# GpSimd's gather, token numbers and low parts of w1 in another order and with fewer waits, and TensorE's instruction pages ended at chosen places

## The chip, the cores and the metric

The kernel runs on one core of one Trainium2 chip. A core has five engines that run side by side, each with its own list of instructions, and that wait for each other through semaphores: TensorE (PE in the profile; its weight loads are PEld), VectorE (DVE), ScalarE (ACT), GpSimd (POOL) and SyncE (SP), which here only starts transfers. The metric is the time of one execution on the device in microseconds; less is better.

## What is computed

Attention in chunks of 64 keys, then a mixture of experts with two levels of routing. `N` is 4608 tokens, `D` 512, `F` 1024; there are 4 groups of 4 experts.

```python
scores = scale * (q_c @ k_c.T)              # per batch, head and chunk of 64
attn = softmax(scores);  x = attn @ v_c     # x becomes [4608, 512]
g_idx = argmax(x @ w_group);  g_w = softmax(x @ w_group)[g_idx]
e_idx = argmax(x @ w_expert[g_idx]);  e_w = softmax(...)[e_idx]
h = maximum(x @ w1[g, e], 0)
out = g_w * e_w * (h @ w2[g, e])            # each token by its one expert
```

## The kernel before

**Two halves.** The first half is one straight list of instructions for each engine, written by a recorder (`Recorder`), that finds by itself which instruction must wait for which; the second half is a loop over blocks of up to 256 tokens of one expert. In the profile every recorded instruction has the line of the recorder's `play`, L309, so the first half is told apart by tiles.

**The first half** handles 36 tiles of 128 tokens in a software pipeline. In turn t TensorE computes the scores of tile t+1 (`b`, tiles `qk`), transposes the exponentials of tile t-1 (`c`, tile `pr`), takes every second turn products for the router (`xT` with `wg`, or `lt` with `cs`), computes the weighted sum of tile t-2 (`p`, tiles `va` and `pT`) and transposes x of tile t-3 (`x`). VectorE normalises a tile's x (`n`: `rc`, then x), subtracts the maximum (`s`: `m`, then `pr`) and does the routing in pieces (`more`). The last turns and what is added to single turns stand in two tables of letters, `TAIL` and `EXTRA`.

**GpSimd** has three kinds of work here. It writes the token numbers into the last columns of x, one column for each tile (`tensor_copy`, CAST in the profile). It scatters the rows of x by expert into the DRAM array `xs`, one indirect DMA for each tile (L752; tiles come in groups of four, a group has one of the buffers `xl`, `x0`, `x1`, `x2`, used again four groups later). And it prepares the first expert: it starts the loads of its w1 and w2 (letter F, `w1r` and `w2r`), gathers its first 256 tokens from `xs` into `xg0r` (F2 and F3), and computes the low parts of w1 (letter P, eight pieces, `w1l` = `w1r` - `w1h`; ScalarE writes `w1h` just before).

**What the recorder makes wait.** All of `xs` is one entry in the recorder's book. A scatter counts as a reader of the entry, a gather as a writer:

```python
def scatter_x(pos, g, i):
    R.gpsimd.do(..., [pos, x, ("xs", (0, 1, 0, 1))], [], "s%d" % (g % 4), g)
...
R.gpsimd.do(lambda e: e.dma_start(xg0[:, j, :], xs[ds(st["r", j], P), :]),
            [], [xg0[:, j, :], ("xs", (0, 1, 0, 1))], "g%d" % j)
```

So a gather waits for all scatters in front of it in the list, the second gather for the first, and every later scatter for the second gather, each until the transfer has landed. GpSimd works through its list in order.

**TensorE's list** of the first half has 1810 entries. An f32 product takes four instruction slots (two passes, each a weight load and a matmul), a transpose or a product of another type two, a wait that stands alone one. The list runs through without regard to where a block of 256 slots ends.

Of the kernel before, what the change touches and what calls it, by code (L numbers as in the profile page):

```python
# [19 lines left out]
P = 128  # L20
# [26 lines left out]
EXTRA = {3: "C0", 4: "Z0", 5: "Z1", 6: "Z2", 7: "Z3", 8: "Z4",  # L47
         24: "F0", 25: "F1", 27: "P0 P1", 28: "F4", 29: "F2 F3", 30: "P2 P3 F5", 31: "P4 P5 P6"}
TAIL = ("b34 n30 s33 c32 m1 p31 m2 e33 x30 b35 n31 s34 m1 c33 P7 p32 m2 e34 x31 36 n32 s35 B0 c34 p33 17 e35 m1 n33 x32 27 W0"
        " p34 c35 n34 B1 m2 W1 x33 W2 p35 n35 m2 x34 X0 x35 X1 m3 R0 R1 37 18 m3 y0 y1 y2 W3 W4 W5 W6 W7 y3 R2 y4 y5 y6 L0 28 m2 m1 L1 m4 H0 y7"  # L50
# [63 lines left out]
BASE, TOP = 16512, 229376  # L114
LATE = 25600


class Op:
    def __init__(self, eng, fn, lane):
        self.eng, self.fn, self.lane, self.waits, self.inc = eng, fn, lane, [], False  # L120


class Recorder:
# [4 lines left out]
    def __init__(self, tc):  # L128
        self.tc = tc
        self.ops = {e: [] for e in self.ENGINES}  # L130
        self.seen = {e: {} for e in self.ENGINES}
        self.hist = {}
        self.lanes = {}
        self.alias = {}
        self.live = {}
        for e in self.ENGINES:
            setattr(self, e, Engine(self, e))
# [16 lines left out]

    def add(self, eng, fn, reads, writes, lane=None, group=None):
        op = Op(eng, fn, lane)
        op.plain = False
        op.at = len(self.ops[eng])
        need = []
        acc = [(a, False) for a in reads] + [(a, True) for a in writes]  # L160
# [97 lines left out]
    def wait(self, o, val):  # L258
        return (self.sem[o.eng], o.count) if o.lane is None else (self.sem[o.lane], 16 * val)

    def play(self, name, eng):
        for op in self.ops[name]:
            last = op.waits[-1:] if op.plain else []
            for w in op.waits[:len(op.waits) - len(last)]:
                eng.wait_ge(*self.wait(*w))
            if op.fn is None:
                continue
            z = op.fn(eng)
            for w in last:
                z._wait_ge(*self.wait(*w))  # L270
            if op.lane is not None:
                z.then_inc(self.sem[op.lane], 16)
            elif op.inc:
                z.then_inc(self.sem[name], 1)

# [15 lines left out]
class Engine:  # L291
    def __init__(self, rec, name):
        self.rec, self.name = rec, name

    def do(self, fn, reads=(), writes=(), lane=None, group=None):
        return self.rec.add(self.name, fn, list(reads), list(writes), lane, group)

    def __getattr__(self, op):
        def f(*args, **kw):
            named = dict(kw)  # L300
            lane, group = named.pop("lane", None), named.pop("group", None)
            aps = lambda z: [a for a in z if hasattr(a, "tensor") and hasattr(a, "ap")]
            if "out" in named:
                writes, reads = [named["out"]], aps(args) + aps(v for k, v in named.items() if k != "out")
            else:
                writes, reads = [args[0]], aps(args[1:]) + aps(named.values())
            reads = [a for a in reads if a.space != DRAM]
            writes = [a for a in writes if a.space != DRAM]
            z = self.do(lambda e: getattr(e, op)(*args, **named), reads, writes, lane, group)  # L309
            z.plain = True  # L310
            return z
        return f
# [3 lines left out]
def moe_kernel(tc, qk, v, wgs, w1, w2, cst, out):  # L316
# [4 lines left out]
    with ExitStack() as ctx:  # L321
# [114 lines left out]
        with ExitStack() as c1:  # L436
# [87 lines left out]
            def stage_b(t):  # L524
                s = st.setdefault(t, {})
                T = st["T", t // 2][:, t % 2]
                sc = scb[t % 2]
                for hp in range(4):
# [30 lines left out]
            def stage_pv(t):  # L559
                s = st[t]  # L560
                pT = s["pT"]
                W = HD + 1
                o = scb[0] if t == NT - 2 else ob
                for hp in range(4):
                    for x, c, rows, cols in TILES:
# [3 lines left out]
            def stage_norm(t):  # L569
# [10 lines left out]
                if i == 0:  # L580
                    st["x", g] = xl if g % 4 == GL % 4 else xbufs[g % 4 - 1]
                R.gpsimd.tensor_copy(st["x", g][:, i, D:D + 1].bitcast(I32), cs[:, C_TID + t:C_TID + t + 1])
                x = st["x", g][:, i, 0:D]
# [214 lines left out]
            def first_loads(i):  # L798
# [873 lines left out]
```

## Time and profile before

| | |
|---|---|
| median of 3 runs | 624.8 us (624.0 to 625.17) |
| profiled execution | 627.61 us, its span 626.0 us |
| PE busy | 583.8 us, 93% |
| DVE, ACT, POOL busy | 364.3, 263.1, 161.2 us |
| mean granted TensorE clock | 0.968 of full speed |
| data moved | 128.24 MB, mean 205 GB/s |

The span runs from the first to the last instruction of the profiled execution; 1.6 us of its time lie around it. The first half, with attention and routing, ends at about 172 us; the loop over experts takes the rest. Busy shares are means over both. An engine counts as busy while an instruction runs on it; "idle before" is the time in front of an instruction in which its engine ran nothing, and the name behind it is what ended that time. "issue" stands for idle time for which no other engine and no transfer is found. The granted clock is given as a share of 2.4 GHz; in this trace it is 1.0 or 0.5 at any one time.

### The profile page before, as it was taken

The page shows a single profiled execution, that of the slowest core. Times are in us where ns is not written, and L with a number is a line of the kernel's source. Part 1 is how long each engine was busy: PE and PEld are TensorE (multiplying, and loading weights), DVE is VectorE, ACT ScalarE, POOL GpSimd, SP SyncE. Part 2 cuts the span into 40 slices and gives each one's busy share as a digit, 9 for nine tenths or more (in the row PEclk, how much of TensorE's full clock was granted, in tenths as well). Part 3 has the DMA queues.
Part 4 walks back from the last instruction along what each step waited for, and adds up shares of the span by engine and source line. Part 5 has one row for each costly group of instructions (what it writes and reads, how often), then busy time and mean ns, then how long its engine had stood idle before and what let it go on. Part 6 is the DMA issues. An engine that isn't in the chain of part 4 may idle for free.

```text
span 626.0 us, 16004 instructions
## 1 busy us (share of the span) xinstructions
PE 583.8 (93%) x5711; PEld 503.1 (80%) x5712; DVE 364.3 (58%) x688; ACT 263.1 (42%) x367; POOL 161.2 (26%) x279
## 2 busy tenths in 40 slices
PE   6897989957899999989999999999999999999995
PEld 4766767745779799878889899989989988898984
DVE  4586769863876672127497674725525578854311
ACT  2464445743444461125475362625215365552111
POOL 0002324348342311221333212221111124311120
PEclk9798889985999999999999999999999999999999
DMA  8987997729639984115489954451712686931110
GB/s 299 422 278 258 372 363 229 228 77 286 173 108 323 328 300 171 68 30 200 142 298 339 301 191 180 171 206 63 281 50 89 238 317 206 339 102 67 34 38 30
DMA packets 43103, 128.24 MB, mean 205 GB/s; under 512 B 4590, under 2 KB 4974, under 8 KB 41136
## 3 DMA queue, kind: packets, MB, share of 16 engines
q1 hardware_dynamic: 32192, 93.93, 43.4%
q0 software_dynamic: 10864, 33.64, 15.3%
q8 instruction: 35, 0.57, 0.4%
q14 instruction: 12, 0.10, 0.0%
HBM read 106.40 MB, written 21.93 MB: 205 GB/s over the span
## 4 chain that ended last, share of the span: by engine, by line
PE 77%; DMA 10%; DVE 5%; issue 4%; POOL 2%; SPq 1%; ACT 1%; POOLq 0%; ACTq 0%; DVEq 0%
PE banks L1109 29%; PE banks L1094 22%; PE banks L309 14%; PE banks L1078 5%; DMA xs<-xl,pos 3%; DMA w1r<-in_moe_w_dram 2%; DMA xgr<-xs 2%; PE banks L994 2%; DMA out_dram<-xl,io__154 1%; DMA qk<-in_qk_dram 1%; PE banks L1040 1%; PE banks L1063 1%; PE banks L1010 1%; DVE big L309 1%; DVE m L309 1%
## 5 line engine op out<-in xcount | busy, mean ns | idle before, releaser
L1094 PE MATMUL banks<-big,w1h 128*128 128x256 f32 x896 | 128.1, 283 | 1.6 <-issue 1.6
L1094 PEld LDWEIGHTS banks<-big,w1h 128*128 128x128 f32 x896 | 117.3, 192 | 3.0 <-issue 2.0
L1255 ACT ACTIVATE big<-banks 128x512 fp32r<-128x512 f32 x58 | 34.5, 597 | 158.6 <-PE banks L1094 105.3
L1109 PE MATMUL banks<-big,big 128*128 128x512 f32 x360 | 84.6, 393 | 0.0
L1585 POOL DMA_INDIRECT out_dram<-xl,io__154 x37 | 41.1, 1111 | 154.8 <-DVE xl L1321 144.0
L1109 PEld LDWEIGHTS banks<-big,big 128*128 128x128 f32 x360 | 66.5, 188 | 14.4 <-ACT big L1305 0.7
L1354 DVE SCALAR_TENSOR_TENSOR big<-banks,big 128x512 fp32r<-128x512 f32 x54 | 36.1, 687 | 64.5 <-ACT big L1255 64.1
L1094 PE MATMUL banks<-big,w1l 128*128 128x256 f32 x448 | 72.3, 283 | 0.6 <-DVE w1l L1331 0.6
L1109 PE MATMUL banks<-w2h,big 128*128 128x512 f32 x288 | 71.2, 393 | 1.5 <-ACT big L1255 1.4
L1331 DVE TENSOR_TENSOR w1l<-w1r,w1h 128x2048 fp32r<-128x2048 f32 x28 | 63.1, 2290 | 16.1 <-ACT w1h L1242 14.3
L1321 DVE TENSOR_SCALAR xl<-banks,io__154 128x512 f32<-128x512 f32 x33 | 24.7, 748 | 67.5 <-PE banks L1109 66.0
L1109 PEld LDWEIGHTS banks<-w2h,big 128*128 128x128 f32 x288 | 53.1, 188 | 13.0 <-ACT big L1255 1.8
L1094 PEld LDWEIGHTS banks<-big,w1l 128*128 128x128 f32 x448 | 61.9, 192 | 0.8 <-DVE w1l L1331 0.8
L1242 ACT CAST w1h<-w1r 128x2048 fp32r<-128x2048 f32 x28 | 52.1, 1903 | 6.7 <-DMA w1r<-in_moe_w_dram 4.9
L309 PE MATMUL banks<-va,pT 64*64 64x65 f32 x1152 | 30.0, 247 | 13.9 <-DVE x L309 6.9
L309 PEld LDWEIGHTS banks<-va,pT 64*64 64x64 f32 x1152 | 24.2, 154 | 23.2 <-DVE x L309 7.9
L309 PE MATMUL banks<-qk 64*64 64x64 f32 x1152 | 29.4, 233 | 11.6 <-issue 7.8
L309 PEld LDWEIGHTS banks<-qk 64*64 64x64 f32 x1152 | 23.0, 141 | 20.2 <-issue 11.0
L1335 DVE TENSOR_TENSOR w2l<-w2r,w2h 128x1024 fp32r<-128x1024 f32 x32 | 37.1, 1218 | 1.8 <-ACT w2h L1274 1.2
L309 ACT COPY pT<-banks 128x512 f32<-128x512 f32 x36 | 21.1, 585 | 36.4 <-PE banks L309 35.8
L1109 PE MATMUL banks<-w2l,big 128*128 128x512 f32 x144 | 35.6, 389 | 0.0
L752 POOL DMA_INDIRECT xs<-x,pos x24 | 24.8, 1033 | 39.7 <-DVE pos L309 27.0
(218 smaller groups left out, 898.6 us busy)
## 6 DMA issues: line engine op xcount, KB each, us to landing
w1r<-in_moe_w_dram SPq DMA_DIRECT2D x30, 1024.0 KB
w2r<-in_moe_w_dram SPq DMA_DIRECT2D x30, 1024.0 KB
qk<-in_qk_dram SPq DMA_DIRECT2D x15, 1024.0 KB, 15.3
xgr<-xs POOLq DMA_DIRECT2D x38, 257.0 KB, 5.2
va<-in_v_dram SPq DMA_DIRECT2D x24, 390.0 KB
qk<-in_qk_dram SPq DMA_DIRECT2D x6, 512.0 KB, 8.6
w1r<-in_moe_w_dram POOLq DMA_DIRECT2D x2, 1024.0 KB, 9.7
w2r<-in_moe_w_dram POOLq DMA_DIRECT2D x2, 1024.0 KB, 7.2
```

Of the source, the lines that this page charges most:

```text
L309: z = self.do(lambda e: getattr(e, op)(*args, **named), reads, writes, lane, group)
L752: R.gpsimd.do(lambda e: e.indirect_dma_start(xs, bass.IndirectOffsetOnAxis(ap=pos, axis=0), x, None), [pos, x, ("xs", (0, 1, 0, 1))], [], ...
L1078: m = pe.matmul(ph[n], a_[:, c, 0:P], w_[:, c, n * 512:(n + 1) * 512], start=(i == 0), stop=(i == 11))
L1094: m = pe.matmul(ph[f // 2][:, f % 2 * 256:f % 2 * 256 + 256], w_[:, c, f * P:(f + 1) * P], a_[:, c, :], start=(i == 0), stop=(i == 11))
L1109: m = pe.matmul(py[j], a_[:, f, half[j]], w_(b, f), start=(i == 0), stop=(i == 23))
L1242: lambda b, s, j: ac.copy(wt[b][0][:, s], w1r[j]), K1)
L1255: ac.activation(hth()[:, 2 * b:2 * b + 2, :], ph[b].rearrange("p (f t) -> p f t", f=2), AF.Relu).then_inc(S["Ha"], 1)
L1321: return ve.tensor_scalar(out=yb[:, j, :], in0=py[j], scalar1=io_[:, j, 1:2], scalar2=None, op0=ALU.mult)
L1331: lambda b, s, j: ve.tensor_sub(wt[b][1][:, s], w1r[j], wt[b][0][:, s].bitcast(F32)), K1, js)
L1335: m = ve.tensor_sub(wt[b][4 + 2 * j + i], w2r[j][:, 2 * i:2 * i + 2], wt[b][2 + j][:, 2 * i:2 * i + 2].bitcast(F32))
L1354: ve.scalar_tensor_tensor(out=htl()[:, 2 * b:2 * b + 2, :], in0=ph[b].rearrange("p (f t) -> p f t", f=2), scalar=0.0, in1=hth()[:, 2 * b:2 ...
L1585: gp.indirect_dma_start(out, bass.IndirectOffsetOnAxis(ap=io[:, j, 0:1].bitcast(I32), axis=0), yb[:, j, :], None, bounds_check=N - 1, oob_ ...
```

## The change

1. **The book of `xs` has two entries.** The transfers that fill `xs` with padding write "zeros"; a scatter reads "zeros" and its own group's entry in "rows". A gather for the first expert no longer stands in the book; it waits for the scatters of groups 0 to 3 by name (`after=`), and nobody waits for it through `xs`.
2. **One copy of token numbers for each group**, of four columns, at the group's first tile, in place of four.
3. **The eight P pieces are dealt out** one or two to a turn (`EXTRA`, `TAIL`); each goes with ScalarE's copy in front of it.
4. **TensorE's list is cut into pages** (`Pages`). A page ends in front of a score stage or a weighted sum that has a wait, if one lies in the last 64 slots of a page of 256, else where 256 slots are full less one. At a cut an instruction `addr_align` puts what follows at the next multiple of 256 slots. The first page has 191 slots, since other instructions stand ahead of the list.

```diff
-         24: "F0", 25: "F1", 27: "P0 P1", 28: "F4", 29: "F2 F3", 30: "P2 P3 F5", 31: "P4 P5 P6"}
+         24: "F0", 25: "F1", 27: "P0", 28: "P1 F4", 29: "F2 F3 P2", 30: "P3 F5", 31: "P4"}
...
+PAGE, FIRST, SLACK = 256, 191, 64
...
-    def add(self, eng, fn, reads, writes, lane=None, group=None):
+    def add(self, eng, fn, reads, writes, lane=None, group=None, after=()):
...
-        need = []
+        need = list(after)
...
+class Pages:
+    def __init__(self, pe, rec):
+        self.pe = pe
+        size = lambda op: getattr(op, "cost", 0) + max(0, len(op.waits) - 1 if op.plain else len(op.waits))
+        ops, self.pages, at, room = rec.ops["tensor"], [], 0, FIRST
+        while at < len(ops):
+            n, i, cut = 0, at, None
+            while i < len(ops) and n + size(ops[i]) <= room:
+                if i > at and ops[i].stage and ops[i].waits:
+                    cut = i, n
+                n += size(ops[i])
+                i += 1
+            if i < len(ops):
+                if cut and cut[1] > room - SLACK and cut[1] < room:
+                    i, n = cut
+                else:
+                    while n > room - 1:
+                        i -= 1
+                        n -= size(ops[i])
+            self.pages.append((ops[at:i], room - n))
+            at, room = i, PAGE
+    def play(self, emit):
+        for k, (ops, left) in enumerate(self.pages):
+            for op in ops:
+                emit(op)
+            if k + 1 < len(self.pages):
+                self.pe.addr_align(PAGE, offset=0, max_nops=0)
...
+                z.cost = 4 if op == "matmul" and named["lhsT"].dtype == F32 else 2
...
+                R.tensor.stage("b%d" % t)
...
+                R.tensor.stage("p%d" % t)
...
-                R.gpsimd.tensor_copy(st["x", g][:, i, D:D + 1].bitcast(I32), cs[:, C_TID + t:C_TID + t + 1])
+                    R.gpsimd.tensor_copy(st["x", g][:, :, D].bitcast(I32), cs[:, C_TID + t:C_TID + t + NG])
...
-                            [pos, x, ("xs", (0, 1, 0, 1))], [], "s%d" % (g % 4), g)
+                            [pos, x, ("zeros", (0, 1, 0, 1)), ("rows", (g, g + 1, 0, 1))], [], "s%d" % (g % 4), g)
...
-                    R.gpsimd.do(lambda e: e.dma_start(xg0[:, j, :], xs[ds(st["r", j], P), :]), [], [xg0[:, j, :], ("xs", (0, 1, 0, 1))], "g%d" % j)
+                    R.gpsimd.do(lambda e: e.dma_start(xg0[:, j, :], xs[ds(st["r", j], P), :]), [], [xg0[:, j, :]], "g%d" % j,
+                                after=[o for o, b, _ in R.hist["rows"] if b[0] <= GC])
...
-                R.sync.do(lambda e: e.dma_start(xs[i * P:(i + 1) * P, :], pad), [pad], [("xs", (0, 1, 0, 1))], "z%d" % j)
+                R.sync.do(lambda e: e.dma_start(xs[i * P:(i + 1) * P, :], pad), [pad], [("zeros", (0, 1, 0, 1))], "z%d" % j)
...
-                    R.play("tensor", pe)
+                    Pages(pe, R).play(lambda op: R.emit("tensor", pe, op))
```

In the `TAIL` table P5, P6 and P7 now stand behind x30, x31 and x32 (P7 stood behind c33). The line numbers of recorded instructions become those of the code that records them; that changes nothing on the chip.

**GpSimd around the gathers**, before, from the first scatter of group 4 (buffer `xl`) on:

```order
L752 DMA xs<-xl,pos_0_120 75904x514
L309 CAST x_98<-cs 128x1
L418 DMA w2r_90<-in_moe_w_dram 128x4x512
L752 DMA xs<-xl,pos_1_125 75904x514
L309 CAST x_98<-cs 128x1
L801 TENSOR_LOAD xi_68
L812 ISA
L812 DMA xg0r<-xs 128x514
L801 TENSOR_LOAD xi_68
L812 ISA
L812 DMA xg0r<-xs 128x514
L752 DMA xs<-xl,pos_2_130 75904x514
```

In the changed kernel, from the second scatter of group 4 on:

```order
L801 DMA xs<-xl,pos_1_125 75904x514
L852 TENSOR_LOAD xi_68
L861 ISA
L861 DMA xg0r<-xs 128x514
L852 TENSOR_LOAD xi_68
L861 ISA
L861 DMA xg0r<-xs 128x514
L481 TENSOR_TENSOR w1l_87<-w1r_89,w1h_86 128x512
L801 DMA xs<-xl,pos_2_130 75904x514
L481 TENSOR_TENSOR w1l_87<-w1r_89,w1h_86 128x512
L463 DMA w2r_91<-in_moe_w_dram 128x4x512
L801 DMA xs<-xl,pos_3_131 75904x514
```

The two gathers keep their place behind the second scatter of `xl`; one low part of w1 now stands behind them and one between the third and the fourth scatter, and the casts of single columns are gone.

**TensorE at tiles 9 to 11** (the scores of a tile are the rows of `qk`, the weighted sums those of `va` with `pT`), before:

```order
L309 MATMUL banks<-cs,x_98 128x128 x4
L309 MATMUL banks<-qk_85 64x64 x16
L309 MATMUL banks<-cs,pr_106 128x128 x4
L309 MATMUL banks<-cs,lt_100 128x20 x2
L309 MATMUL banks<-va_95,pT_104 64x65 x16
L309 MATMUL banks<-cs,x_98 128x128 x4
L309 MATMUL banks<-qk_73 64x64 x16
L309 MATMUL banks<-cs,pr_103 128x128 x4
L309 MATMUL banks<-xT_109,wg 32x256 x4
L309 MATMUL banks<-va_95,pT_107 64x65 x16
```

The same place in the changed kernel, where ISA is a cut:

```order
L645 MATMUL banks<-cs,x_98 128x128 x4
L314 ISA
L578 MATMUL banks<-qk_85 64x64 x16
L602 MATMUL banks<-cs,pr_106 128x128 x4
L672 MATMUL banks<-cs,lt_100 128x20 x2
L615 MATMUL banks<-va_95,pT_104 64x65 x16
L645 MATMUL banks<-cs,x_98 128x128 x4
L578 MATMUL banks<-qk_73 64x64 x16
L602 MATMUL banks<-cs,pr_103 128x128 x4
L665 MATMUL banks<-xT_109,wg 32x256 x4
L314 ISA
L615 MATMUL banks<-va_95,pT_107 64x65 x16
```

No product has moved; a cut stands in front of one tile's scores and of another tile's weighted sum. The whole list has 25 cuts. Counted with the slot sizes above, 1 to 54 slots stay empty at each, 19 in the mean.

## Rows read from the trace of the kernel before

**Rows 1.** Busy us (instructions) of each engine, granted clock, DMA share, GB/s, by stage
```profile
core 0: us, PE busy (x) PEld busy (x) DVE busy (x) ACT busy (x) POOL busy (x), PEclk, DMA share, GB/s
...
15.00:55.00 40.00, 35.03 (x835) 27.21 (x826) 27.98 (x86) 21.13 (x43) 1.44 (x10) 0.90 0.86 322
55.00:95.00 40.00, 34.74 (x742) 26.44 (x745) 25.82 (x90) 18.04 (x39) 13.07 (x22) 0.89 0.99 349
...
131.00:161.00 30.00, 18.51 (x238) 13.48 (x238) 13.77 (x48) 10.55 (x20) 19.65 (x26) 0.66 0.67 202
...
210.00:626.00 416.00, 406.51 (x2531) 363.88 (x2529) 220.66 (x243) 161.96 (x181) 93.60 (x173) 1.00 0.50 173
```

**Rows 2.** POOL in order of time: start us, us, work [idle before <- what ended it]
```profile
117.25 1.02 POOL L752 DMA_INDIRECT xs<-xl,pos  x1 [0.30 <-DVE m L309]
...
126.24 0.57 POOL L812 DMA_DIRECT2D xg0r<-xs  x1 [7.77 <-DMA xs<-xl,pos]
130.22 0.56 POOL L812 DMA_DIRECT2D xg0r<-xs  x1 [3.41 <-DMA xg0r<-xs]
133.89 1.03 POOL L752 DMA_INDIRECT xs<-xl,pos  x1 [3.11 <-DMA xg0r<-xs]
...
135.08 2.48 POOL L309 TENSOR_TENSOR w1l<-w1r,w1h 128x512 fp32r<-128x512 f32 x2
137.51 0.79 POOL L418 DMA_DIRECT2D w2r<-in_moe_w_dram  x1
138.60 1.03 POOL L752 DMA_INDIRECT xs<-xl,pos  x1 [0.30 <-issue]
```

**Rows 3.** DVE in order of time, 121 to 147 us
```profile
121.35 0.12 DVE L309 TENSOR_REDUCE pos<-ps 128x1 int32<-128x16 f32 x1
...
131.98 0.12 DVE L309 TENSOR_REDUCE pos<-ps 128x1 int32<-128x16 f32 x1
135.15 2.43 DVE L309 TENSOR_TENSOR x<-gt 128x4 f32<-128x4 f32 x1 [3.06 <-POOL x L309]
...
145.81 0.69 DVE L309 TENSOR_TENSOR xl<-banks,rc 128x512 f32<-128x512 f32 x1 [4.06 <-DMA xs<-xl,pos]
```

**Rows 4.** PE in order of time, 138 to 162 us
```profile
138.24 1.15 PE L309 MATMUL banks<-va,pT 64*64 64x65 f32 x32 [5.85 <-DVE x L309]
...
146.56 1.15 PE L309 MATMUL banks<-va,pT 64*64 64x65 f32 x32 [3.72 <-DVE xl L309]
...
161.01 0.74 PE L309 MATMUL banks<-big,w1h 128*128 128x256 f32 x4
```

**Rows 5.** PE in order of time, 53 to 59 us, after a long stall
```profile
53.75 1.10 PE L309 MATMUL banks<-va,pT 64*64 64x65 f32 x32
...
57.99 0.70 PE L309 MATMUL banks<-va,pT 64*64 64x65 f32 x32
58.62 0.66 PE L309 MATMUL banks<-cs,x 128*128 128x128 f32 x4
```

**Rows 6.** Whom PE waited for, 0 to 130 us: us in total, times, longest
```profile
PE banks L309 <- issue: 10.6, 14, 2.0
```

**Rows 7.** The chain that ended last, 40 to 88 us: start us, us, what
```profile
40.63 9.70 PE banks L309 x254
50.34 1.99 issue
...
80.69 4.49 PE banks L309 x127
85.17 1.92 issue
```

**Rows 8.** The DMA queue of instructions, 15 to 130 us: packets, MB, share
```profile
q8 instruction: 19, 0.31, 1.0%
```

**Rows 9.** The chain that ended last, 117 to 158 us
```profile
117.25 8.31 DMA xs<-xl,pos
...
138.60 7.12 DMA xs<-xl,pos
...
147.97 9.34 PE banks L309 x100
```

More of the change, by code (lines that the diff above doesn't have):

```diff
@@ L1 @@
+import sys
 from contextlib import ExitStack
@@ L47 @@
 EXTRA = {3: "C0", 4: "Z0", 5: "Z1", 6: "Z2", 7: "Z3", 8: "Z4",
-         24: "F0", 25: "F1", 27: "P0 P1", 28: "F4", 29: "F2 F3", 30: "P2 P3 F5", 31: "P4 P5 P6"}
-TAIL = ("b34 n30 s33 c32 m1 p31 m2 e33 x30 b35 n31 s34 m1 c33 P7 p32 m2 e34 x31 36 n32 s35 B0 c34 p33 17 e35 m1 n33 x32 27 W0"
+         24: "F0", 25: "F1", 27: "P0", 28: "P1 F4", 29: "F2 F3 P2", 30: "P3 F5", 31: "P4"}
+TAIL = ("b34 n30 s33 c32 m1 p31 m2 e33 x30 P5 b35 n31 s34 m1 c33 p32 m2 e34 x31 P6 36 n32 s35 B0 c34 p33 17 e35 m1 n33 x32 P7 27 W0"
         " p34 c35 n34 B1 m2 W1 x33 W2 p35 n35 m2 x34 X0 x35 X1 m3 R0 R1 37 18 m3 y0 y1 y2 W3 W4 W5 W6 W7 y3 R2 y4 y5 y6 L0 28 m2 m1 L1 m4 H0 y7"
@@ L115 @@
 LATE = 25600
+PAGE, FIRST, SLACK = 256, 191, 64
 class Op:
     def __init__(self, eng, fn, lane):
-        self.eng, self.fn, self.lane, self.waits, self.inc = eng, fn, lane, [], False
+        self.eng, self.fn, self.lane, self.waits, self.inc, self.stage = eng, fn, lane, [], False, None
 class Recorder:
@@ L134, in __init__ @@
         self.alias = {}
+        self.stage = None
         self.live = {}
@@ L153, in box @@
         return p0, p0 + dims[0][1], lo * size, hi * size
-    def add(self, eng, fn, reads, writes, lane=None, group=None):
+    def add(self, eng, fn, reads, writes, lane=None, group=None, after=()):
         op = Op(eng, fn, lane)
+        op.stage, self.stage = self.stage, None
         op.plain = False
         op.at = len(self.ops[eng])
-        need = []
+        need = list(after)
         acc = [(a, False) for a in reads] + [(a, True) for a in writes]
@@ L259, in wait, with emit @@
         return (self.sem[o.eng], o.count) if o.lane is None else (self.sem[o.lane], 16 * val)
+    def emit(self, name, eng, op):
+        last = op.waits[-1:] if op.plain else []
+        for w in op.waits[:len(op.waits) - len(last)]:
+            eng.wait_ge(*self.wait(*w))
+        if op.fn is None:
+            return
+        with self.tc.nc.source_location(__file__, op.line):
+            z = op.fn(eng)
+        for w in last:
+            z._wait_ge(*self.wait(*w))
+        if op.lane is not None:
+            z.then_inc(self.sem[op.lane], 16)
+        elif op.inc:
+            z.then_inc(self.sem[name], 1)
     def play(self, name, eng):
         for op in self.ops[name]:
[L263 to L274, printed above, removed]
+            self.emit(name, eng, op)
+class Pages:
[25 more added lines that the diff above has]
+                self.pe.addr_align(PAGE, offset=0, max_nops=0)
 class Memory:
@@ L293, in __init__, with stage, do @@
         self.rec, self.name = rec, name
-    def do(self, fn, reads=(), writes=(), lane=None, group=None):
-        return self.rec.add(self.name, fn, list(reads), list(writes), lane, group)
+    def stage(self, name):
+        self.rec.stage = name
+    def do(self, fn, reads=(), writes=(), lane=None, group=None, line=None, after=()):
+        z = self.rec.add(self.name, fn, list(reads), list(writes), lane, group, after)
+        z.line = line or sys._getframe(1).f_lineno
+        return z
     def __getattr__(self, op):
@@ L308, in f @@
             writes = [a for a in writes if a.space != DRAM]
-            z = self.do(lambda e: getattr(e, op)(*args, **named), reads, writes, lane, group)
+            z = self.do(lambda e: getattr(e, op)(*args, **named), reads, writes, lane, group, sys._getframe(1).f_lineno)
             z.plain = True
+            if self.name == "tensor":
+                z.cost = 4 if op == "matmul" and named["lhsT"].dtype == F32 else 2
             return z
```

## The prediction

> **What bounds the kernel now.** I read the stages first [rows 1]. From 210 us on TensorE is busy 406.5 of 416 us at full clock: the expert loop is bound by TensorE and takes as long as it takes, so whatever the first half gains or loses moves the end by the same amount. In the first half two stages stand out. From 131 to 161 us TensorE is busy 18.5 of 30 us, and the granted clock is 0.66, a mix of the two levels 1.2 and 2.4 GHz. From 15 to 95 us it is busy 69.8 of 80 us at a clock of 0.90 and 0.89. The change touches both.
>
> The stage from 131 us is read in the timelines of three engines. GpSimd [rows 2] starts a scatter at 117.25 and then does nothing until 126.24, where the first gather goes: it waited 7.8 us for that scatter to land. The second gather waits 3.4 us for the first, the next scatter 3.1 us for the second, and stands at 133.89. The fourth scatter of `xl` follows at 138.60. VectorE had the rows' places ready long before: the fourth scatter's are the `pos` at 121.35 [rows 3]. VectorE pays twice: at 135.15 it had waited 3.1 us for GpSimd's token numbers (its write into a gate column of x lies between them), and the normalisation at 145.81 had waited 4.1 us until the fourth scatter of `xl` had landed, because it writes the same buffer. TensorE pays with it [rows 4]: 5.85 us in front of the weighted sum at 138.24 and 3.72 us in front of that at 146.56. What it runs in between goes at half clock: the weighted sum takes 1.15 us there and 0.70 at 57.99 [rows 4, 5].
>
> The stalls of the earlier stage have "issue" as their releaser, 10.6 us in 14 pieces [rows 6]. In the chain that ended last [rows 7] they come after 127 matmuls, or 254, with as many weight loads: 254 instructions or twice that, a block of 256 less a few waits. One packet of 16 KB on the queue "instruction" goes with each, 19 in 115 us [rows 8]. So TensorE stalls where a block of instructions ends and the next has not come. Some time after the long stall at 50.34 [rows 7] the clock stood at half for a while: 1.10 us for a weighted sum [rows 5].
>
> **The gather and the token numbers.** Removed are the three waits on GpSimd, 7.77 + 3.41 + 3.11 = 14.3 us [rows 2]. The scatters that the gathers still wait for, groups 0 to 3, all stand ahead of the first of `xl`, at least two turns earlier. From 118.3 us, where the second scatter of `xl` ends, I count on: two gathers with the loads of their row numbers, about 1.1 us each by 0.57 and as much again in front of it; one P, half of 2.48, so 1.24; the third scatter 1.03; one P 1.24; the load of w2 0.79; with gaps of 0.3 [rows 2] the fourth scatter starts near 125.5, an estimate, where it stood at 138.60. Its landing took 7.1 us (138.60 to 145.7), and 8.3 us for the one at 117.25 [rows 9]. So `xl` is free at 132.6 to 133.8.
>
> What is late next? VectorE has the places of a tile ready at 131.98 [rows 3] and its normalisation into x from 132.1 on, now without waiting, then the maximum and the subtraction of another tile, 0.69 each, and reaches the normalisation into `xl` near 134.3. That is 11.5 us before 145.81, and the landing is just out of the way, by about a microsecond. From 145.81 to the first product of the first expert at 161.01 lie 15.2 us. A run of 9.3 us in it [rows 9] was at half clock nearly to its end; by 0.70 to 1.15 for a weighted sum [rows 4, 5] it shrinks by 0.4 of itself, so about 4 us less. I keep 2.5 of it, since VectorE's and ScalarE's pieces for the last tiles then end last more often. That makes 14 us. From this goes what the P pieces cost: each holds GpSimd 1.24 us, and the VectorE operation at 135.15 took 2.43 us beside two of them [rows 2, 3], where operations of that size take some 0.2. Five of the eight now fall in turns in which VectorE is busy nearly all the time; I take 0.5 us for the lot, since only few operations are of that kind. **Sum: 13.5 us.** Bounds: below, the two waits on TensorE alone, 5.85 + 3.72 = 9.6 us [rows 4]; above, the stage run by TensorE alone at full clock: the busy 18.5 us [rows 1] lose some 5.5 of the 14 us that ran at half clock, 13 us remain, and 30 - 13 gives 17.
>
> The three casts fewer for each group lay beside other work; they are worth nothing, since GpSimd was busy 13 of 40 us even at 55 to 95 us [rows 1]. A copy of four columns must wait for all four scatters of the group four before; these went some three turns of 3 us earlier, more than the 7 to 8 us of landing, so it holds nobody, but if a landing took 4 us more the scatters behind it on GpSimd would wait. ScalarE's copies go with the P pieces: two or three less in one turn, one more in the next, nothing. The loads of w1 for the loop start when the last P has read its buffer; that comes earlier by what GpSimd gains, and their time is not on the path.
>
> **The pages.** At stake are the 10.6 us of stalls and the half clock that follows some of them. The clock of 0.90 and 0.89 means 8 and 9 us at half speed [rows 1], which loses 40% of each, some 7 us. Does ending a page in front of a wait take the stall away? What I see is a race: the block is asked for once, and comes after a time; the page before it must last that long. The 19 blocks in 115 us [rows 8] are one in 6.05 us, less 0.56 of stall: a page lasts 5.5 us. The change makes a page shorter by 19 of 256 slots, 0.4 us less of cover. If every turn were late, that would cost 20 x 0.4 = 8 us. Against that stands what TensorE has in hand when the block's end is reached: in front of a cut lie four transposes of 0.66 us together [rows 5], or router products, where in the middle of a weighted sum there lie 32 in 0.70. If the engine is handed instructions ahead of the work, some eight slow ones cover half a microsecond of a stall, eight quick ones 0.1; by 14 stalls at most 7 us. And where TensorE would have waited for VectorE anyway, the stall lies inside that wait; but TensorE is busy 87% of this stage with the stalls counted in [rows 1], so there is little to lie inside. The two sides cancel; **I take 0**, with -13 (nearly all stalls and their half clock gone, the VectorE then being the bound) and +8 as bounds.
>
> The Trainium skill, page "Runtime: NRT & Kernel Launch", section "Instruction fetch mechanics", says that crossing such a block costs one bump of a DMA queue's tail and is mostly hidden. Up to 1.99 us per turn in this trace [rows 7] speak against it; by that rule the pages would be worth 0 as well, and the sum would be the same 13.5. The same section says that a taken branch to a block outside the two at hand forces a fetch before anything goes on. The block behind a cut is the next one, which by the rule is at hand or on its way; if it were thrown away it would be the third rival below.
>
> **The sum.** 626.0 - 13.5 = 612.5 us of span, 614.1 us for the profiled execution (1.6 around the span). The median of the runs stands 2.8 us under the profiled 627.61; so **611.3 us**.
>
> **Rivals.**
> *The pages pay.* TensorE's turns fall into waits and the clock stays up: up to 13 us more, 598 us; half of it, 605. For it: the stalls in the middle of scores are the longest, 1.99 and 1.92. Against: so few waits for VectorE.
> *The pages cost, or the tail gains less.* Shorter pages meet blocks that come no faster: +8, 619 us. Or the landing of the fourth scatter is late, or the spread P pieces hold the scatters and VectorE back, and only 5 us of the 13.5 come: 620 us. For it: that landing has a microsecond to spare, and the DMA engines were nearly full at 55 to 95 us, share 0.99 [rows 1].
> *The cuts break the stream: slower.* Place: each of some 20 cuts before 130 us. If the jump over the empty slots makes the sequencer ask anew for the block, every turn costs what the worst cost, 1.99 us [rows 7], in place of 0.56: 20 x 1.4 = 29 us, 624.8 - 13.5 + 29 = 640 us, more with the half clock. It decides from 0.7 us more per turn on, where the 13.5 us are eaten. Against: the instruction behind the jump is the next block's first, which the stream would have brought next.
> *The cuts miss.* If a page's count were wrong by a slot, a cut would stand just behind a block's start and leave a nearly empty block, a further fetch for each. Against: the stalls come after 127 and 254 matmuls, as the slot sizes say [rows 7].
>
> **How the numbers follow.** The forecast (605 to 617) 0.56; the pages pay (597 to 605) 0.14; the pages cost or the tail gains less (617 to 623) 0.18, of which 0.02 ends within the bound of no change; cuts break the stream or miss 0.12, of which 0.09 is slower and 0.03 lands near the old time. The range must leave no more than 0.2 out: 600 to 621 holds the forecast, some three fifths of the first rival and nearly all of the second, 0.81. What a measurement of this kernel can tell from no change is 0.2%, 1.25 us: faster 0.86, same 0.05, slower 0.09.
>
> **What will show it.** GpSimd's gathers right behind the second scatter of `xl`, a few tenths apart, and the fourth scatter near 125 us; the weighted sums of the last tiles without 5.85 and 3.72 us in front; the first expert's first product 12 to 16 us earlier than 161.0 relative to the tile scores; the granted clock near 1.0 from 135 us on. For the pages: the "issue" total before 130 us against 10.6, and whether the idle time stands at the cuts. If "issue" is far under 5 us the first rival holds, over 15 the second or third. I am wrong if TensorE's wait comes back under another name (a landing, a low part of w1), or if the loop's start does not move with the first product.

## The result

| | before | changed |
|---|---|---|
| median of 4 runs each | 624.98 us (624.0 to 626.44) | 617.08 us (614.34 to 618.63) |
| profiled execution | 627.61 us, span 626.0 | 618.42 us, span 616.8 |
| mean granted TensorE clock | 0.968 | 0.982 |

By the medians the changed kernel is 7.9 us faster. The ratio on record is 0.9851, with a 95% interval of 0.9818 to 0.9883. The ratios on record leave out runs over 1.5% above the fastest of their kernel, and they are not the quotients of the medians printed beside them (here 0.9874). The forecast was 611.3 us, 13.5 us faster, in a range of 600 to 621, with 605 to 617 as its main case. 617.08 lies at the edge of that case, where the rival "the pages cost, or the tail gains less" begins. The sign and the mechanism on GpSimd came true, and the gain was 5.6 us smaller than the sum said.

### The profile page after: what moved, and what is told of

Same layout as the page of the kernel before. It is cut to its first block, busy times and chain, and to the rows that moved or that the text cites. A ratio compares the mean times of both kernels' runs of the same rounds, so it can differ in the third digit from the quotient of the medians.

```text
span 616.8 us, 16000 instructions
## 1 busy us (share of the span) xinstructions
PE 579.8 (94%) x5711; PEld 498.9 (81%) x5712; DVE 360.8 (58%) x688; ACT 263.3 (43%) x367; POOL 158.2 (26%) x252
## 3 DMA queue, kind: packets, MB, share of 16 engines
q0 software_dynamic: 10864, 33.64, 15.5%
## 4 chain that ended last, share of the span: by engine, by line
PE 71%; DVE 11%; DMA 7%; issue 5%; POOL 2%; SPq 1%; ACT 1%; another core or an unknown queue 0%; DVEq 0%; POOLq 0%; ACTq 0%
PE banks L1159 28%; PE banks L1144 22%; PE banks L1128 4%; PE banks L615 2%; DVE x L633 2%; DVE pr L590 2%; DMA xgr<-xs 2%; DVE m L586 2%; DMA w1r<-in_moe_w_dram 2%; DMA qk<-in_qk_dram 2%; PE banks L471 2%; PE banks L602 2%; PE banks L1044 2%; PE banks L645 1%; PE banks L578 1%
## 5 line engine op out<-in xcount | busy, mean ns | idle before, releaser
L1159 PE MATMUL banks<-w2h,big 128*128 128x512 f32 x288 | 72.6, 399 | 0.2 <-ACT big L1305 0.2
L578 PE MATMUL banks<-qk 64*64 64x64 f32 x1152 | 27.8, 232 | 12.5 <-DMA qk<-in_qk_dram 3.5
L578 PEld LDWEIGHTS banks<-qk 64*64 64x64 f32 x1152 | 22.3, 141 | 20.8 <-DVE pr L590 4.5
L615 PEld LDWEIGHTS banks<-va,pT 64*64 64x64 f32 x1152 | 21.4, 141 | 16.5 <-issue 4.8
L801 POOL DMA_INDIRECT xs<-x,pos x24 | 24.2, 1008 | 40.3 <-DVE pos L810 21.7
L1629 POOL COPY in__155<-xgr 128x2 int32<-128x2 int32 x22 | 10.7, 485 | 92.6 <-PE banks L1044 78.7
```

What stands on the lines that cost most here:

```text
L578: R.tensor.matmul(sc[cols, x, hp * CH:hp * CH + CH], lhsT=T[rows, 0, hp, cols], rhs=T[rows, 1, hp, cols], start=True, stop=True)
L615: R.tensor.matmul(o[cols, x, hp * W:hp * W + W], lhsT=pT[rows, hp, cols], rhs=v_at(2 * t + c)[rows, hp], start=True, stop=True)
L1159: m = pe.matmul(py[j], a_[:, f, half[j]], w_(b, f), start=(i == 0), stop=(i == 23))
```

## The profile after

The trace is read at three milestones that both kernels have: the scores of the last tile on TensorE, the first normalisation into `xl` on VectorE (135.65 us now; 145.81 in [rows 3]), and the first product of the first expert (161.01 in [rows 4]). Recorded instructions now carry the lines of the code that records them: L578 scores, L615 weighted sum, L633 normalisation, L801 scatter, L861 gather, L481 low part of w1, L471 first product.

GpSimd of the changed kernel in order of time (start us, us, work, idle before and what ended it); it answers [rows 2]:

```profile
117.70 1.00 POOL L801 DMA_INDIRECT xs<-xl,pos  x1 [0.30 <-DVE gt L747]
118.71 1.15 POOL L861 DMA_DIRECT2D xg0r<-xs  x2
119.84 1.32 POOL L481 TENSOR_TENSOR w1l<-w1r,w1h 128x512 fp32r<-128x512 f32 x1
121.34 1.03 POOL L801 DMA_INDIRECT xs<-xl,pos  x1 [0.18 <-DVE ps L785]
122.39 1.30 POOL L481 TENSOR_TENSOR w1l<-w1r,w1h 128x512 fp32r<-128x512 f32 x1
123.62 0.79 POOL L463 DMA_DIRECT2D w2r<-in_moe_w_dram  x1
124.72 1.01 POOL L801 DMA_INDIRECT xs<-xl,pos  x1 [0.30 <-issue]
125.73 0.20 POOL L631 CAST x<-cs 128x4 int32<-128x4 f32 x1
```

Both gathers go right behind the second scatter of `xl`, without the waits of 7.77 and 3.41 us, and the fourth scatter starts at 124.72 instead of 138.60. VectorE of the changed kernel, some rows in order of time; they answer [rows 3]:

```profile
125.97 0.69 DVE L633 TENSOR_TENSOR x<-banks,rc 128x512 f32<-128x512 f32 x1 [2.42 <-POOL x L631]
...
135.65 0.69 DVE L633 TENSOR_TENSOR xl<-banks,rc 128x512 f32<-128x512 f32 x1
...
142.78 0.68 DVE L633 TENSOR_TENSOR xl<-banks,rc 128x512 f32<-128x512 f32 x1
...
145.66 0.17 DVE L622 TENSOR_SCALAR rc<-banks 128x8 f32<-128x8 f32 x1 [1.50 <-PE banks L869]
...
146.10 0.69 DVE L633 TENSOR_TENSOR xl<-banks,rc 128x512 f32<-128x512 f32 x1
```

The normalisation into `xl` no longer waits for a landing. A new wait stands at 125.97: x waits 2.42 us for the merged copy of token numbers, which GpSimd does at 125.73, behind a low part of w1, the load of w2 and a scatter. TensorE of the changed kernel, some rows; they answer [rows 4]:

```profile
126.71 0.70 PE L615 MATMUL banks<-va,pT 64*64 64x65 f32 x32 [1.51 <-DVE x L633]
...
131.42 0.69 PE L578 MATMUL banks<-qk 64*64 64x64 f32 x32 [0.19 <-DVE pr L590]
...
146.85 0.96 PE L645 MATMUL banks<-cs,xl 128*128 128x128 f32 x4 [2.39 <-DVE xl L633]
...
151.01 1.22 PE L471 MATMUL banks<-big,w1h 128*128 128x256 f32 x4
```

The waits of 5.85 and 3.72 us are gone. The new one of 1.51 is the merged copy's (it ends 0.05 us behind x, 125.97 + 0.69), and 2.39 us stand in front of the last transposes of `xl`. The first product starts at 151.01, but takes 1.22 us where it took 0.74. The first half by stages (the row from 131 to 161 us now holds 10 us of the loop), with the last two rows split at the milestones (length, then busy us and instructions of PE, PEld, DVE, ACT, POOL, then the granted clock, the DMA share, GB/s); they answer [rows 1]:

```profile
15.00:55.00 40.00, 33.80 (x887) 26.41 (x887) 28.38 (x86) 21.27 (x45) 0.73 (x4) 0.96 0.91 335
55.00:95.00 40.00, 33.79 (x771) 25.59 (x764) 27.65 (x96) 18.11 (x40) 12.41 (x15) 0.91 0.99 351
...
131.00:161.00 30.00, 24.98 (x315) 19.83 (x313) 21.43 (x80) 16.11 (x31) 14.50 (x14) 0.89 0.68 207
...
131.42:135.65 4.23, 3.20 (x79) 2.46 (x80) 3.38 (x17) 3.24 (x7) 2.24 (x2) 1.00 0.42 78
135.65:151.01 15.36, 11.57 (x160) 7.57 (x160) 9.23 (x37) 8.20 (x16) 7.83 (x9) 0.87 0.74 237
```

**Where the time went.** Four stretches give the difference of the two spans:

| us | before | after | difference |
|---|---|---|---|
| start to the last tile's scores | 131.07 | 131.42 | +0.35 |
| first leg: to the first normalisation into `xl` | 14.74 | 4.23 | -10.51 |
| second leg: to the first product | 15.20 | 15.36 | +0.16 |
| first product to the end | 465.0 | 465.8 | +0.8 |
| span | 626.0 | 616.8 | -9.2 |

The first leg brought all of it. The second leg, which the sum let shrink, kept its length. The rest between 9.2 and the medians' 7.9 is that the profiled execution stood 2.6 us over the median of its four runs before and 1.3 us after.

**The stall that changed its name.** TensorE's idle time before 130 us of the changed kernel by what ended it (us in total, times, longest), two groups of several; they answer [rows 6]:

```profile
PE banks L615 <- issue: 1.9, 2, 1.6
...
PE banks L578 <- issue: 1.2, 3, 0.4
```

"issue" fell from 10.6 to 3.1 us. But all idle time of TensorE from 15 to 130 us, summed over all releasers, was 12.3 us before and 17.6 after. Its busy time in this stretch fell by 4.3 us (102.43 to 98.13) at a granted clock of 0.96 in place of 0.93, so the last tile's scores come only 0.35 us later. Three cuts of the changed kernel, TensorE in order of time:

```profile
27.79 0.69 PE L578 MATMUL banks<-qk 64*64 64x64 f32 x32 [1.41 <-DVE m L586]
...
72.30 0.69 PE L578 MATMUL banks<-qk 64*64 64x64 f32 x32 [1.50 <-DVE pos L810]
...
79.15 0.70 PE L615 MATMUL banks<-va,pT 64*64 64x65 f32 x32 [1.62 <-issue]
```

Packets on the queue "instruction" start at 25.39, 69.85 and 76.70 us; TensorE goes on 2.40, 2.45 and 2.45 us behind each, whatever name the wait has. At eight cuts the distance is 2.40 to 2.54 us. A cut in front of a wait puts the stall behind an instruction that also waits for a semaphore, and the profile then names the semaphore's owner. That the block is what is late there is read from this distance; the view that groups the waits hides it. The time at which the named work ended is the second test. The `pos` named at 72.30 had ended at 71.64 (71.52 + 0.12), 0.66 us before TensorE went on.

The distance alone does not settle it: the wait that ends at 126.71 stands 2.48 us behind a packet at 124.23, and it is the merged copy's. In the second trace of the changed kernel the same wait again ends 0.05 us behind x, but 1.98 us behind its packet.

## The experiments

The kernels ran in three groups of four, each group on one chip together with the kernel before, whose median was 624.56 us on the first chip, 619.96 on the second and 626.17 on the third. Ratios are to the kernel before on the same chip.

**Are the pages or GpSimd's part the gain?** Four kernels on the first chip. The changed kernel without pages:

```diff
-                    Pages(pe, R).play(lambda op: R.emit("tensor", pe, op))
+                    R.play("tensor", pe)
```

> The changed kernel without its pages: TensorE's list runs through as before; the parts on GpSimd stay. Theory A (a block of instructions is asked for when the one before it is entered, and the place where it ends does not matter): the whole gain stays, 6 to 11 us under the kernel before, and within 2 us of the changed kernel. Theory B (ending a block in front of a wait hides the turn, and part of the 7.9 us comes from there): only 2 to 5 us under the kernel before.

Measured: 614.78 us, ratio 0.9829 (0.9800 to 0.9858). All of the gain is there without the pages.

Pages alone: the kernel before with `Pages`, and with the old book, tables and copies. Against the changed kernel (the old tables and copies are those of the next diff; the gather and the padding go back to the entry "xs" in the same way):

```diff
-                            [pos, x, ("zeros", (0, 1, 0, 1)), ("rows", (g, g + 1, 0, 1))], [], "s%d" % (g % 4), g)
+                            [pos, x, ("xs", (0, 1, 0, 1))], [], "s%d" % (g % 4), g)
...
```

> The kernel before with the pages alone; GpSimd as before. Theory A: within 3 us of the kernel before on either side; the idle time that stood as issue before 130 us (10.6 us) now stands in front of scores and weighted sums, 10 to 16 us. Theory B: 3 to 8 us faster.

Measured: 627.19 us, 1.0050 (1.0023 to 1.0077): 2.6 us slower, within the 3 us of Theory A. The first leg is 13.88 us here, as before: VectorE of this kernel has the old wait,

```profile
143.38 0.69 DVE L633 TENSOR_TENSOR xl<-banks,rc 128x512 f32<-128x512 f32 x1 [3.60 <-DMA xs<-xl,pos]
```

The book alone: the kernel before with the entries "zeros" and "rows" and `after=`, no pages, single columns, the P pieces in their old turns. Against the kernel without pages:

```diff
-         24: "F0", 25: "F1", 27: "P0", 28: "P1 F4", 29: "F2 F3 P2", 30: "P3 F5", 31: "P4"}
+         24: "F0", 25: "F1", 27: "P0 P1", 28: "F4", 29: "F2 F3", 30: "P2 P3 F5", 31: "P4 P5 P6"}
...
-                    R.gpsimd.tensor_copy(st["x", g][:, :, D].bitcast(I32), cs[:, C_TID + t:C_TID + t + NG])
+                R.gpsimd.tensor_copy(st["x", g][:, i, D:D + 1].bitcast(I32), cs[:, C_TID + t:C_TID + t + 1])
...
```

> The kernel before with the two-entry book of xs alone: the gathers wait for the scatters of groups 0 to 3 by name, nothing waits for the gathers through xs; copies, P pieces and TensorE's list as before. If the gathers' waits were the cause of the stall at 131 to 161 us: 7 to 11 us faster than before, first product of the first expert near 150 us. If the spread P pieces carry a good part: under 5 us faster.

Measured: 619.08 us, 0.9908 (0.9877 to 0.9940), 5.5 us of gain. That lies between the two expectations (7 to 11, and under 5). The first leg is 4.99 us, and the first product stands at 150.34.

Shorter pages: every page ends 64 slots early, wherever that falls.

```diff
-                if cut and cut[1] > room - SLACK and cut[1] < room:
-                    i, n = cut
-                else:
-                    while n > room - 1:
+                if True:
+                    while n > room - 64:
```

> The changed kernel with each page ended 64 slots early, wherever that falls: 192 slots in a block of 256. Theory A: a page lasts 3.9 us in place of 4.9 at full clock and a block still takes 5 to 6 us, so nearly every turn before 130 us stalls 1 to 2 us: 12 to 25 us slower than the changed kernel. Theory B, or a block that comes in good time when the load of the queues allows: under 6 us slower.

Measured: 641.31 us, 1.0241 (1.0207 to 1.0275), 26.5 us over the kernel without pages on the same chip. TensorE's waits before 130 us:

```profile
PE banks L576 <- issue: 11.8, 5, 4.0
PE banks L613 <- issue: 11.3, 7, 3.2
```

and the clock falls with them, 0.80 and 0.78 in two stages:

```profile
55.00:95.00 40.00, 31.45 (x645) 24.12 (x643) 23.16 (x80) 15.72 (x35) 8.32 (x10) 0.80 0.77 275
95.00:131.00 36.00, 30.23 (x627) 23.70 (x619) 23.43 (x93) 15.28 (x33) 9.77 (x12) 0.78 0.62 205
```

So the race that the prediction describes is real: a shorter page covers less. By this row the rule that a crossing is mostly hidden, which the prediction cites from the Trainium skill ("Runtime: NRT & Kernel Launch", "Instruction fetch mechanics"), does not hold for this stream.

**Does the place or the length of a page count, and does the jump cost?** Two kernels on the second chip: the jump without shorter pages (`SLACK = 0`: a cut only where 256 slots less one are full), and pages 19 slots shorter anywhere (as above, with `room - 19`).

```diff
-PAGE, FIRST, SLACK = 256, 191, 64
+PAGE, FIRST, SLACK = 256, 191, 0
```

> The changed kernel with pages that end only where a block of 256 is full (1 to 4 slots left empty), so the cut and its jump are there but hardly a slot is lost. Theory A (length alone counts): as the run without pages, ratio 0.983 plus or minus 0.003. If the jump itself costs, some 0.1 us or more at each of 24 cuts: 0.987 or more, slower than the changed kernel.

Measured: 612.91 us (607.65 to 618.20), 0.9876 (0.9819 to 0.9932). The two kernels without any cut on this chip (below) took 611.91 and 611.86, with ratios of 0.9865 and 0.9860. By its number the result meets the "0.987 or more" of a jump that costs, but on this chip the kernels without a jump stand almost there too. The jump has no price that can be seen; 0.1 us at each of 24 cuts would not be seen either, since these intervals leave room for some 4 us.

> The changed kernel with every page ended 19 slots early, wherever that falls: as many slots lost in the mean as in the changed kernel, the cuts anywhere. Theory A (the place does not matter): as the changed kernel, 0.985 plus or minus 0.003. Theory B (in front of a wait the turn is partly hidden): 3 us or more slower than the changed kernel, 0.990 or more.

Measured: 615.51 us, 0.9934 (0.9904 to 0.9964). By its number Theory B's "0.990 or more" is met. It is 2.6 us over the full pages, with intervals that overlap, and 3.6 us over the two kernels without cuts, with intervals that hardly touch. The changed kernel had not run beside it, so it ran again, on the third chip, beside one with its own page lengths at other places:

```diff
+        full = [sum(size(o) for o in p) for p, _ in self.pages]
+        full = full[:1] + full[-2:0:-1] + [1 << 30]
+        self.pages, at = [], 0
+        for want in full:
+            i, n = at, 0
+            while i < len(ops) and n + size(ops[i]) <= want:
+                n += size(ops[i])
+                i += 1
+            self.pages.append((ops[at:i], 0))
+            at = i
```

> The changed kernel once more, as the measure for the three kernels that run on the same chip with it. Both theories: 0.985 of the kernel before, as on its first chip (interval 0.982 to 0.988).

Measured: 617.78 us, 0.9864 (0.9831 to 0.9897).

The kernel with moved cuts:

> The changed kernel with the same page lengths dealt out in the opposite order: the first page keeps its 191 slots, the pages behind it take the lengths that the changed kernel's pages have from the last but one back to the second. The number of pages and the empty slots stay the same, but nearly all cuts now stand inside scores, weighted sums or transposes instead of in front of them. Theory A (what a page costs is its length; the place of the cut is worth nothing): 0.985, within 1.5 us of the changed kernel on this chip. Theory B (shorter pages cost, and a cut in front of a wait gives a part of that back): 0.991 to 0.995, 4 to 6 us slower than the changed kernel, with idle time behind the cuts that is put down to issue, 9 us or more before 130 us.

Measured: 615.79 us, 0.9841 (0.9798 to 0.9883). With the cuts inside scores and sums it is not slower, 2 us on the faster side with overlapping intervals; Theory B's 0.991 to 0.995 lies outside the interval, so it falls here. TensorE's idle time from 15 to 130 us was 15.5 us, of it 12.9 "issue"; in the changed kernel's second trace 12.8, of it 2.4 "issue". The name moves, the time does not follow it.

The kernel without pages, on this chip:

> The changed kernel without pages, on the chip of the changed one. Theory A and B alike: the pages as a whole give nothing, so 0.983, 0 to 3 us faster than the changed kernel here. Rival (the pages pay, and the first comparison was one of two chips): 0.988 or more, at least 2 us slower than the changed kernel.

Measured: 617.73 us, 0.9863 (0.9826 to 0.9900), within 0.1 us of the changed kernel. The rival, that the pages pay, finds no support: here the intervals leave some 3 us either way, and on the first chip the pages alone were slower than the kernel before.

**What do the spread low parts and the merged copy do?** The book alone once more, on the third chip:

> The kernel before with the new book of xs alone (no pages, token numbers by single columns, low parts of w1 in their old turns), on the same chip as the kernel with all of GpSimd's part. Theory C (spreading the low parts of w1 over the turns is worth a third or more of the gain, since three of them in a row hold up GpSimd's scatters and so the last normalisations): 0.990, 4 to 5 us slower than the kernel without pages. Rival D (the book is the gain, the spread is worth under 1 us, as the prediction has it): within 1.5 us of the kernel without pages, 0.983 to 0.985.

Measured: 619.99 us, 0.9898 (0.9861 to 0.9935): 2.3 us over the kernel without pages here, 4.3 us on the first chip. The ratio is Theory C's 0.990, the difference lies between the two expectations. The sign was the same twice; here the intervals overlap, on the first chip they lie apart (0.9877 to 0.9940 against 0.9800 to 0.9858). The trace shows how it comes about. GpSimd of this kernel in order of time:

```profile
127.15 3.70 POOL L481 TENSOR_TENSOR w1l<-w1r,w1h 128x512 fp32r<-128x512 f32 x3
131.02 1.01 POOL L801 DMA_INDIRECT xs<-x,pos  x1 [0.17 <-DVE one L707]
```

its VectorE in the same stretch:

```profile
127.41 3.54 DVE L707 TENSOR_TENSOR one<-lg,mx 128x80 f32<-128x80 f32 x1
...
131.77 0.68 DVE L633 TENSOR_TENSOR x<-banks,rc 128x512 f32<-128x512 f32 x1
```

and its TensorE behind it:

```profile
132.51 1.14 PE L615 MATMUL banks<-va,pT 64*64 64x65 f32 x32 [3.58 <-DVE x L633]
```

Three low parts in a row hold GpSimd for 3.70 us where the changed kernel has one at a time. VectorE's `one` (one of its routing pieces, else 0.24 us long) starts among them and ends 0.1 us behind the last of them; x comes behind it, and TensorE waits 3.58 us for x. In the book alone on the first chip the same operation takes 3.61 us and TensorE waits 3.62. The four traces with the low parts in their old turns all have VectorE operations of this kind, 1.28 to 3.61 us long, each of which ends 0.02 to 0.11 us behind the run of low parts that it met; in the ten traces with the low parts spread, no VectorE operation ahead of the first product takes over 0.69 us. The kernel without pages, which differs from the book alone by the spread and the merged copy, reaches the last tile's scores 3.1 us earlier here (131.55 against 134.63) and 3.9 us earlier on the first chip (127.67 against 131.58); that the copy is not what gains is shown next. Spreading the low parts alone was not run.

The merged copy was undone or moved on the second chip, in the kernel without pages. Four single columns again:

```diff
-                    R.gpsimd.tensor_copy(st["x", g][:, :, D].bitcast(I32), cs[:, C_TID + t:C_TID + t + NG])
+                R.gpsimd.tensor_copy(st["x", g][:, i, D:D + 1].bitcast(I32), cs[:, C_TID + t:C_TID + t + 1])
```

> The changed kernel without its pages and with four copies of one column for each group, as before; the two-entry book and the spread P pieces stay. The merged copy made VectorE wait 1.7 and 0.9 us for GpSimd near 122 and 136 us in the run without pages (2.4 and 0.8 in the changed kernel). If that wait is on the path: 1 to 3 us under the run without pages (ratio 0.979 to 0.982 to the kernel before). If it is hidden: the same ratio, 0.983 plus or minus 0.002. If fewer copies help by themselves: slower than the run without pages.

Measured: 611.91 us, 0.9865 (0.9822 to 0.9909).

The merged copy one tile earlier, ahead of that tile's scatter:

```diff
+                if t % NG == NG - 1 and t < TL:
+                    u = t // NG + 1
+                    nx = xl if u % 4 == GL % 4 else xbufs[u % 4 - 1]
+                    R.gpsimd.tensor_copy(nx[:, :, D].bitcast(I32), cs[:, C_TID + t + 1:C_TID + t + 1 + NG])
...
```

> The changed kernel without its pages, the merged copy kept but given to GpSimd one tile earlier, ahead of that tile's scatter. If the wait of 1.7 and 0.9 us for the copy is on the path: 1 to 3 us under the run without pages, and no wait of VectorE for GpSimd's copy in the trace. If hidden: the same, ratio 0.983 plus or minus 0.002.

Measured: 611.86 us, 0.9860 (0.9817 to 0.9902). Neither trace has VectorE waiting for GpSimd's copy in the last tiles. The expected ratios were set against the first chip's 0.983, and this group has no kernel without pages that keeps the copy in its place; the nearest is the one with full pages, which still has the wait (612.91; VectorE waits 1.68 us for the copy there). Neither kernel is measurably faster than that. The wait is real, and no cost of it can be seen; these intervals would hide one of some 4 us.

## Why the prediction was right, and what it mis-sized

**The bound and the place: right.** The loop took 465.0 and 465.8 us from the first product on, so what the first half gained moved the end.

**GpSimd's waits: right.** Forecast for the fourth scatter near 125.5, found 124.72. With the book alone the first leg is already 4.99 and 5.32 us, so the book, which frees the gathers, removes the wait of 4.06 us [rows 3] and most of what stood ahead of it. With pages and the old book the leg is 13.88 us and the wait 3.60.

**The first leg: 1 us too much.** VectorE reached `xl` at 135.65, not 134.3; it did so without waiting, as forecast. The term is 10.5 us in place of 11.5.

**The second leg: the term that failed.** The step was that 15.2 us behind the first normalisation into `xl` shrink by about 4 as the clock rises, of which 2.5 were kept because VectorE and ScalarE would end last more often. Measured +0.16. The two parts can be told apart: in the stretch 135.65 to 151.01 TensorE was busy 11.57 us; the same leg of before, with the columns of [rows 1], is

```profile
145.81:161.01 15.20, 13.00 (x156) 9.39 (x156) 7.90 (x30) 6.54 (x13) 8.39 (x14) 0.66 0.82 256
```

So the clock gave back 1.4 us, and TensorE's idle time rose from 2.2 to 3.8. Two things stand in it: the wait of 2.39 us at 146.85, and the half clock that follows. TensorE had been busy 1.52 of the 4 us before 147 at a granted clock of 1.00, and from there on the clock was 0.51, which is the level of 1.2 GHz for nearly all of the stretch:

```profile
143.00:147.00 4.00, 1.52 (x40) 1.25 (x30) 2.40 (x11) 2.75 (x6) 1.73 (x2) 1.00 0.79 154
147.00:151.00 4.00, 4.00 (x23) 2.04 (x22) 2.80 (x11) 1.07 (x2) 0.16 (x1) 0.51 0.60 244
```

What the term would have been at full clock stands in the traces of the second chip. The same leg of the kernel with pages 19 slots shorter there, 135.78 to 147.32, by the columns of [rows 1]:

```profile
135.78:147.32 11.54, 9.88 (x159) 6.89 (x159) 7.88 (x30) 7.81 (x16) 7.64 (x8) 1.00 0.76 242
```

and TensorE's last transposes of `xl` in it:

```profile
144.85 0.66 PE L643 MATMUL banks<-cs,xl 128*128 128x128 f32 x4 [0.48 <-DVE xl L631]
```

11.54 us, 3.7 less than before: 3.1 of it is TensorE's busy time, 0.5 its idle time. The 4 us that the prediction worked out from the clock, before it kept 2.5, come near the 3.1. But this leg has a second advantage, which the clock does not explain: from the third to the fourth normalisation into `xl` it takes 1.78 us there, 3.32 in the changed kernel's trace and 3.40 before (last section). So how much a leg at full clock and without that advantage would have gained is not shown. The four kernels on that chip have 11.4 to 12.6; the kernels with the new book on the other chips have 13.8 to 16.9. The execution of the changed kernel did not keep the full clock: the wait in front of the last transposes was 2.39 us there and 0.48 here, and the half clock of that trace begins behind it. The other traces agree. Of the twelve that come to this wait at full clock, the five that wait 2.09 to 2.88 us have a first product of 1.15 to 1.22 us behind it, the seven that wait 0.48 to 1.48 us one of 0.74. On that chip the kernel before is faster too (619.96), and the ratio is the same; whether its second leg is shorter there no trace shows.

**The pages: 0 was near, for a reason half right, and so in part by luck.** The race holds (64 slots cost 26.5 us). The other side, that a cut in front of a wait hides part of the stall, has no trace in the times: other places, 2 us faster within the intervals. That 19 slots cost nothing on the third chip, alone 2.6 us on the first and anywhere 3.6 us on the second is the size that is left, 0 to 4 us, where the bound was 8. Why the chips differ is open. The test named for the first rival, "issue" far under 5 us, was met (3.1) and did not mean what I said: it counts a name.

**The merged copy "holds nobody": wrong in the trace, right in the sum.** I looked at the scatters that it must wait for, not at what stands in front of it on GpSimd's queue, nor at who reads or writes its buffer. **The low parts: wrong sign.** I took 0.5 us as the cost of spreading them. Against the old turns with the book already new, spreading them (with the merged copy) is 2.3 and 4.3 us better. I had read the VectorE operation of 2.43 us beside two of them as a price of each low part; it is the price of low parts in a row, and it stood in the kernel before inside the 5.85 us that TensorE waits at 138.24 [rows 4], which I put down to the gathers' waits alone.

**The signs named beforehand.** The gathers, the fourth scatter and the two waits of TensorE came out as told. Two signs failed, both by the second leg: the first product came 10.35 us earlier relative to the last tile's scores (29.94 us before, 19.59 now), not 12 to 16, and the clock behind 135 us was 0.87, not near 1.0. And the sign of being wrong was met in part: a wait of TensorE came back under another name, 2.39 us in front of the last transposes.

**In the sum:** the span came 4.3 us over 612.5: 1.0 from the first leg, 2.7 from the second, 1.15 from the stretches ahead and behind, less the 0.5 for the low parts that the legs hold already. The other 1.5 us up to the median: I took the profiled execution to stand 2.8 us over it, and after the change it stood 1.3 over.

No version beat both kernels beyond the intervals; without the pages the changed kernel is as fast and simpler.

## What to carry to other kernels

Price a removed wait to the next milestone on the engine that ends last, and a hoped-for clock gain behind it as a separate term that may come to nothing. When idle time changes its name, sum all names over the stretch before calling it gone; an idle stretch that ends a fixed time behind an instruction packet (some 2.4 us here) may be the block's, whoever is named, and is, if the named work had ended well before. A wait freed by the book counts in full only when the work behind it on the same queue is spread too: three low parts in a row on GpSimd held a VectorE operation of 0.24 us for 3.54.

## What was not expected of the hardware

From the third to the fourth normalisation into `xl` it takes 3.31 to 3.41 us in the first trace of the changed kernel, in the one of before and in six others, at either clock, 3.56 and 3.82 in two, and 1.77 to 1.78 us in all four traces of the second chip, with the same instructions. In the longer case VectorE gets TensorE's count some 2 us after the recorded end of the weighted sum (142.73 + 0.70, and 145.66), and ScalarE's copy of the transposes that follow (143.52 + 0.66) starts as late, at 145.77. What makes it is open.

Between executions of one kernel the time goes roughly with the mean granted clock: the book alone took 615.12 us at 0.991 and 622.8 at 0.972 on the third chip, in other runs of the same program. It is not the rule everywhere: the changed kernel's fastest run there, 615.77 us, had 0.971, and one of 617.15 had 0.983. A difference of 2 us between two profiled executions is within what one kernel does by itself.
